# Five, four, three and two rows of wo to a transfer in place of three and two

## The chip, the core and the metric

The kernel runs on one core of a Trainium2 chip. The metric is the device time of one launch in microseconds (us), lower is better. The profile gives one execution; the times are medians of unprofiled runs.

## The reference

One decode step for eight sequences: a layer norm, then attention over a cache with grouped heads and a dense Mish block side by side, both added to the input. Everything is float32.

```python
B, Sq, D = 8, 1, 512
Hq, Hkv, Sk, Dh = 32, 8, 8192, 128
xn = layernorm(x)
q = (xn @ wq).reshape(B, 1, 32, 128).transpose(0, 2, 1, 3)
k, v = repeat(k_cache, 4, axis=1), repeat(v_cache, 4, axis=1)
p = softmax(einsum("bhqd,bhkd->bhqk", q, k) * Dh ** -0.5)
o = einsum("bhqk,bhkd->bhqd", p, v)
A = o.transpose(0, 2, 1, 3).reshape(B, 1, 4096) @ wo
act = mish(xn @ w1 + b1)
out = x + A + act @ w2
```

The two caches are 268 MB each; wq and wo are 8 MB each, w1 and w2 3.6 MB each.

## The kernel before

The work is cut into 32 units (`UNITS`): four pairs of KV heads times eight sequences, pair by pair. A unit is one pair of heads of one sequence. Its keys are one transfer of 128 partitions by 64 KB (`load_unit(kT, ...)`, line 140) and its values another of the same size. Both go into the tile `kv`, which has one place for values (`V_AT`) and two places for keys that overlap by half (`K_AT`), so a transfer is issued only when TensorE is through with what stood there before.

The loop over `j` in line 563 is the order of the work; it is written out by hand, and each engine and the queue of SyncE (SP) take their instructions in that order. For a unit `j` it runs half of `scores(j)` (64 matmuls in all, line 329), issues the keys of `j+1`, runs the other half, `softmax(j)`, then `values(j-1)` (line 399), issues the values of `j`, prepares the key weights of `j+1`, and turns the probabilities of `j` for the next round. All loads of the caches, of wq, wo, w1 and w2 are issued by SP, so they stand in one line.

The weights wo are used after the loop. Four groups of wo, one for each pair of heads, come by transfers on 128 partitions (line 612); for the first pair only three of four column blocks come there. The fourth block of the first pair is 32 rows of four pieces of 4 KB, 512 KB in all, and comes during the loop into the tile `ws`, whose earlier content (a part of wq) is used up by then. These transfers are issued by `load_few` (line 485), which the lists `FEW1` and `FEW2` drive. An entry is (first partition, number of rows, first row, unit): in the unit named, after the values of that unit are issued, SP issues that transfer. `FEW1` has eight transfers of three rows in units 22 to 25, two in each, `FEW2` four of two rows in units 28 and 29.

In `load_few` the rows of one transfer lie four apart, in wo and in the tile alike: the transfer that begins at partition `t` fills partitions `t`, `t+4` and `t+8`. The 24 rows of `FEW1` fill partitions 0 to 11 and 32 to 43; the eight of `FEW2` then fill partitions 0 to 7, after `few(0)` (line 511) has used the first 24 at the end of unit 27. `few(1)` uses the last eight after the loop.

After the loop come `values(31)`, `few(1)`, the four groups of wo (`outputs`, line 523), and w2 in five transfers of falling size (`down_long`, line 534, and `down`, line 546), the sum with the input (line 642) and the store (line 643).

Of the kernel before, what the change touches and what calls it, by code (L numbers as in the profile page):

```python
# [65 lines left out]

FEW1 = [(32 * h + t, 3, 12 * h + t, 22 + (4 * h + t) // 2) for h in range(2) for t in range(4)]
FEW2 = [(t, 2, 24 + t, 28 + t // 2) for t in range(4)]  # L70
EARLY = 27


# [4 lines left out]
def kernel(  # L78
# [21 lines left out]
    ws = const.tile([P, CC * BW], F32, name="ws")  # L100
# [381 lines left out]
    def load_few(p, n, q):  # L482

        rows = wo[:4].rearrange("u p f -> (u p f)").rearrange("(u q i f) -> q u i f", u=4, i=4, f=BW)
        nc.sync.dma_start(
            ws[p : p + 4 * n - 3 : 4].rearrange("p (u f) -> p u f", u=4),
            rows[q : q + 4 * n - 3 : 4, :, 3],
        )

    def turn_few():  # L490
# [72 lines left out]
    for j in range(UNITS):  # L563
# [25 lines left out]
        if j == 0:  # L589
            mish(w1_t, b1_sb, kv[:, W1_AT : W1_AT + 6 * FG])  # L590
        for p, n, q, at in FEW1 + FEW2:
            if j == at:
                load_few(p, n, q)
# [14 lines left out]
    for m in range(NP):  # L608
        rows = wo[4 * m : 4 * (m + 1)].rearrange("u p f -> (u p f)")
        rows = rows.rearrange("(p f) -> p f", p=P)  # L610
        n = 3 * BW if m == 0 else 4 * BW
# [4 lines left out]
    for lo, hi in parts:  # L616
        t = kv[:, W2_AT + lo * D : W2_AT + hi * D]
# [64 lines left out]
```

## Time and profile before

| | |
|---|---|
| median of 3 runs | 1310.62 us (1310.28 to 1311.18) |
| the profiled execution's own time | 1310.38 us |
| its span, first to last instruction | 1308.6 us |
| TensorE matmul busy | 987.5 us, 75% |
| VectorE, ScalarE busy | 362.0 us, 39.3 us |
| read from memory | 561.01 MB, 429 GB/s over the span |
| the transfers of the SP queue | 99.3% of sixteen DMA engines' span |
| chain that ended last | DMA 79%, TensorE 20% |
| mean granted TensorE clock | 0.884 |

The span leaves out what lies before the first and after the last instruction, 1.8 us here. The profile counts the time that the packets of a queue took on sixteen DMA engines together, so a share of 99.3% means that on the mean the sixteen were idle for 0.7% of the span; a share of 0.0625 in a short stretch is one engine of the sixteen. TensorE is busy for three quarters of the span and waits for transfers for most of the rest.

### The profile page before, as it was taken

The page shows a single profiled execution, that of the slowest core. Times are in us where ns is not written, and L with a number is a line of the kernel's source. Part 1 is how long each engine was busy: PE and PEld are TensorE (multiplying, and loading weights), DVE is VectorE, ACT ScalarE, POOL GpSimd, SP SyncE. Part 2 cuts the span into 40 slices and gives each one's busy share as a digit, 9 for nine tenths or more (in the row PEclk, how much of TensorE's full clock was granted, in tenths as well). Part 3 has the DMA queues.
Part 4 walks back from the last instruction along what each step waited for, and adds up shares of the span by engine and source line. Part 5 has one row for each costly group of instructions (what it writes and reads, how often), then busy time and mean ns, then how long its engine had stood idle before and what let it go on. Part 6 is the DMA issues. An engine that isn't in the chain of part 4 may idle for free.

```text
span 1308.6 us, 11317 instructions
## 1 busy us (share of the span) xinstructions
PE 987.5 (75%) x5086; PEld 349.0 (27%) x5086; DVE 362.0 (28%) x771; ACT 39.3 (3%) x89; POOL 2.3 (0%) x10
## 2 busy tenths in 40 slices
PE   6967777768878668786878677688796777777677
PEld 4322222223322222232323222232232222222222
DVE  3443022230233332123331232312322330322321
ACT  1000000000000000000000000000000000000000
POOL 0000000000000000000000000000000000000000
PEclk9989888798889899878999888888897898887898
DMA  9999999999999999999999999999999999999997
GB/s 404 441 429 433 433 433 430 431 441 428 435 431 434 433 431 433 431 431 437 425 443 422 443 419 443 429 433 433 426 437 430 438 434 425 441 419 443 423 429 334
DMA packets 11608, 561.80 MB, mean 429 GB/s; under 512 B 1308, under 2 KB 1440, under 8 KB 1960
## 3 DMA queue, kind: packets, MB, share of 16 engines
q1 hardware_dynamic: 11536, 561.06, 99.3%
q8 instruction: 40, 0.66, 0.2%
q14 instruction: 8, 0.07, 0.0%
q10 hardware_dynamic: 24, 0.02, 0.0%
HBM read 561.01 MB, written 0.07 MB: 429 GB/s over the span
## 4 chain that ended last, share of the span: by engine, by line
DMA 79%; PE 20%; issue 0%; SPq 0%; DVE 0%
DMA kv<-in_v 74%; PE o L399 19%; DMA kv<-in_kT 2%; DMA kv<-in_w 2%; DMA kv<-in_wo 2%; PE s L329 1%; PE o L546 0%; SPq L134 0%; DVE os L642 0%
## 5 line engine op out<-in xcount | busy, mean ns | idle before, releaser
L329 PE MATMUL s<-kv,wk 128*64 128x512 f32 x2048 | 502.2, 653 | 180.8 <-DMA kv<-in_kT 180.8
L399 PE MATMUL o<-kv,pt 128*32 128x512 f32 x2048 | 264.5, 675 | 57.4 <-DMA kv<-in_v 57.4
L329 PEld LDWEIGHTS s<-kv,wk 128*64 128x64 f32 x2048 | 164.7, 151 | 495.0 <-issue 413.6
L341 DVE TENSOR_REDUCE nm<-s 128x1 f32<-128x512 f32 x32 | 22.1, 692 | 515.1 <-PE s L329 515.1
L368 PE MATMUL x<-e,perm 128*128 128x512 f32 x256 | 130.1, 655 | 2.0 <-ACT qr L299 2.0
L399 PEld LDWEIGHTS o<-kv,pt 128*32 128x32 f32 x2048 | 69.4, 122 | 226.1 <-issue 175.7
L407 DVE TENSOR_SCALAR os<-o,isel 128x128 f32<-128x128 f32 x32 | 11.2, 351 | 278.2 <-PE o L399 278.2
L379 DVE STREAM_TRANSPOSE tr<-x 128x512 f32<-128x512 f32 x128 | 79.2, 676 | 3.0 <-PE x L368 3.0
L368 PEld LDWEIGHTS x<-e,perm 128*128 128x128 f32 x256 | 50.6, 208 | 74.7 <-issue 72.0
L312 DVE TENSOR_TENSOR wk<-qr,mask 128x512 f32<-128x512 f32 (+1 forms) x66 | 63.5, 1003 | 18.7 <-ACT qr L299 18.7
L360 ACT ACTIVATE e<-s,nmx 128x512 f32<-128x512 f32 x32 | 22.0, 687 | 1119.8 <-DVE nmx L357 1119.8
L388 DVE TENSOR_TENSOR pt<-tr 64x512 f32<-64x512 f32 x64 | 43.9, 686 | 1.6
L384 DVE TENSOR_TENSOR tr<-tr 128x1024 f32<-128x1024 f32 x32 | 39.2, 1226 | 1.1
L409 DVE SCALAR_TENSOR_TENSOR os<-o,isel,os 128x128 f32<-128x128 f32 x96 | 33.7, 351 | 3.4
L342 PE MATMUL m<-ident,nm 128*1 128x128 f32 x32 | 8.6, 270 | 25.3 <-DVE nm L341 25.3
L353 PE MATMUL m<-ident,nx 1*128 1x1 f32 x32 | 7.0, 218 | 24.1 <-DVE nx L349 24.1
L292 PE MATMUL x<-qT,tr 128*128 128x64 f32 x128 | 19.3, 315 | 3.0 <-ACT qr L299 2.7
L292 PEld LDWEIGHTS x<-qT,tr 128*128 128x128 f32 x128 | 18.1, 226 | 6.2 <-ACT qr L299 3.3
L342 PEld LDWEIGHTS m<-ident,nm 128*1 128x1 f32 x32 | 2.5, 79 | 53.5 <-DVE nm L341 53.5
L363 DVE TENSOR_SCALAR lsel<-rsel,l 128x8 f32<-128x8 f32 x32 | 7.4, 231 | 28.8 <-ACT e L360 28.8
L416 PE MATMUL m<-hsel,os 128*128 128x8 f32 x64 | 10.9, 242 | 5.7 <-DVE rt L376 5.7
L416 PEld LDWEIGHTS m<-hsel,os 128*128 128x128 f32 x64 | 10.8, 189 | 15.3 <-issue 8.0
(106 smaller groups left out, 178.8 us busy)
## 6 DMA issues: line engine op xcount, KB each, us to landing
ws<-in_wq SPq DMA_DIRECT2D x4, 2048.0 KB, 22.6
kv<-in_wo SPq DMA_DIRECT2D x3, 2048.0 KB, 24.1
kv<-in_w SPq DMA_DIRECT2D x1, 3584.0 KB, 35.8
kv<-in_wo SPq DMA_DIRECT2D x1, 1536.0 KB
kv<-in_w SPq DMA_DIRECT2D x1, 1280.0 KB
kv<-in_w SPq DMA_DIRECT2D x1, 1024.0 KB
kv<-in_w SPq DMA_DIRECT2D x1, 768.0 KB, 34.9
kv<-in_kT SPq DMA_DIRECT2D x32, 29.4
```

The source lines that it names most:

```text
L292: nc.tensor.matmul(X[:, half, k * 64 : (k + 1) * 64], wide[:, half * 8 + k], qT, start=True, stop=True,)
L312: nc.vector.tensor_mul(w[:, i : i + n, d], q[:, i : i + n, d].to_broadcast([P, n, NH * G, REP]), mask[:, d * NH * G : (d + 1) * NH * G] .r ...
L329: nc.tensor.matmul(S[64 * c : 64 * (c + 1), :], w[:, i].rearrange("p d k h -> p (d k h)"), kk[:, i, c, :], start=(part == 0 and n == 0), s ...
L341: nc.vector.tensor_reduce(nm, S, axis=AX.X, op=ALU.max, negate=True)
L360: nc.scalar.activation(e, S, AF.Exp, bias=nmx, accum_out=l)
L368: nc.tensor.matmul(X[:, g], perm[:, g], e, start=True, stop=True)
L379: nc.vector.transpose(tr.rearrange("p (l t) c -> p t l c", t=TL)[:, tl], X.rearrange("p g (t q l) -> p t l g q", t=TL, q=PP)[:, tl],)
L384: nc.vector.tensor_add(t[:, :, 0], t[:, :, 0], t[:, :, 1])
L388: nc.vector.tensor_add(pt8[half, :, :, d * REP : (d + 1) * REP].rearrange("p c y h -> p y c h"), t[:, 0], t[:, 1],)
L399: nc.tensor.matmul(O[Q * q : Q * (q + 1), :], pt8[:, c, TL * l : TL * (l + 1), :].rearrange("p t h -> p (t h)"), vt[:, 512 * n : 512 * (n ...
L409: nc.vector.scalar_tensor_tensor(os, O[:, DH * i : DH * (i + 1)], isel[:, i : i + 1], os, op0=ALU.mult, op1=ALU.add)
L416: nc.tensor.matmul(M[:, 168 : 168 + H2], os, hsel, start=True, stop=True)
```

## The change

The same 32 rows of the same block of wo come to the same 32 partitions, by nine transfers in place of twelve. `load_few` takes consecutive rows into consecutive partitions, in place of rows four apart. Each twelve rows of `FEW1` come by transfers of five, four and three rows, in units 22 (two), 23 (two) and 24 (two), and the eight rows of `FEW2` by transfers of three, three and two rows in units 28 (two) and 29 (one).

```diff
-FEW1 = [(32 * h + t, 3, 12 * h + t, 22 + (4 * h + t) // 2) for h in range(2) for t in range(4)]
-FEW2 = [(t, 2, 24 + t, 28 + t // 2) for t in range(4)]
+FEW1 = [
+    (32 * h + lo, n, 12 * h + lo, 22 + (3 * h + t) // 2)
+    for h in range(2)
+    for t, (lo, n) in enumerate(((0, 5), (5, 4), (9, 3)))
+]
+FEW2 = [(0, 3, 24, 28), (3, 3, 27, 28), (6, 2, 30, 29)]
 EARLY = 27
...
         rows = wo[:4].rearrange("u p f -> (u p f)").rearrange("(u q i f) -> q u i f", u=4, i=4, f=BW)
         nc.sync.dma_start(
-            ws[p : p + 4 * n - 3 : 4].rearrange("p (u f) -> p u f", u=4),
-            rows[q : q + 4 * n - 3 : 4, :, 3],
+            ws[p : p + n].rearrange("p (u f) -> p u f", u=4), rows[q : q + n, :, 3]
         )
```

The instructions of TensorE, VectorE, ScalarE and GpSimd are the same in the same order; SP issues nine of these transfers where it issued twelve, and all else on its queue keeps its order.

## The prediction

> **What bounds the kernel now.** I read the page first: the slices, the queues and the chain that ended last.
>
> ```profile
> PE   6967777768878668786878677688796777777677
> DMA  9999999999999999999999999999999999999997
> q1 hardware_dynamic: 11536, 561.06, 99.3%
> q8 instruction: 40, 0.66, 0.2%
> DMA 79%; PE 20%; issue 0%; SPq 0%; DVE 0%
> ```
>
> TensorE has gaps in every slice, the DMA engines have none before the last one, and the queue that carries the loads fills 99.3% of sixteen engines' span. So time is what the DMA engines need. But a load counts only when its last engine is through, so it is the slowest engine that matters, not the mean. The stretches of the end show how unequal the sixteen are (us, busy time of TensorE and its loads, VectorE, ScalarE, GpSimd, then the granted clock, the DMA share and GB/s):
>
> ```profile
> 1296.50:1297.50 1.00, 0.89 (x9) 0.26 (x12) 0.00 (x0) 0.00 (x0) 0.00 (x0) 1.00 0.96 381
> 1297.50:1298.50 1.00, 1.00 (x12) 0.12 (x4) 0.00 (x0) 0.00 (x0) 0.00 (x0) 1.00 0.74 311
> 1303.70:1304.00 0.30, 0.04 (x4) 0.04 (x8) 0.00 (x0) 0.00 (x0) 0.00 (x0) 1.00 0.53 205
> 1304.20:1304.40 0.20, 0.20 (x16) 0.20 (x8) 0.00 (x0) 0.00 (x0) 0.00 (x0) 1.00 0.05 20
> 1304.40:1304.60 0.20, 0.20 (x16) 0.11 (x5) 0.00 (x0) 0.00 (x0) 0.00 (x0) 1.00 0.08 31
> 1304.80:1305.00 0.20, 0.20 (x9) 0.00 (x0) 0.00 (x0) 0.00 (x0) 0.00 (x0) 1.00 0.00 0
> ```
>
> About four engines have moved all their bytes at 1298 (share 0.74), eight or nine still run at 1304 (0.53), and from 1304.2 to about 1304.75 only one does (0.05 and 0.08, one of sixteen being 0.0625). The first is 7 us ahead of the last, and the last is 0.55 us behind the next. It decides when the last piece of w2 is whole, and with it the end.
>
> Now the transfers in question, from the DMA view: their sizes, and how many small packets start in short stretches (a packet of wo is 4 KB; the count under 8 KB less that under 512 B, which are completions, gives them). The stretches are 940.28 to 940.59, 940.59 to 940.90, 941.07 to 941.38, and all of 940.25 to 942.4.
>
> ```profile
> ws<-in_wo SPq DMA_DIRECT2D x8, 48.0 KB
> ws<-in_wo SPq DMA_DIRECT2D x4, 32.0 KB
> DMA packets 6, 0.14 MB, mean 449 GB/s; under 512 B 2, under 2 KB 2, under 8 KB 4
> DMA packets 9, 0.15 MB, mean 476 GB/s; under 512 B 3, under 2 KB 3, under 8 KB 7
> DMA packets 8, 0.02 MB, mean 79 GB/s; under 512 B 2, under 2 KB 2, under 8 KB 8
> DMA packets 49, 0.95 MB, mean 442 GB/s; under 512 B 12, under 2 KB 12, under 8 KB 36
> ```
>
> Two, four and six packets start in three stretches of 0.31 us: one engine, then two, then three, each at 0.155 us a packet. The 24 packets of two transfers are three engines times eight. So a transfer of three rows runs on three engines, one row (four packets, 16 KB, 0.62 us) to each, and delays those three and no other. They begin 0.31 and some 0.48 us apart. How far ahead these engines are, the chain of waits tells (start, length, what):
>
> ```profile
> 917.18 29.90 DMA kv<-in_v
> 1189.65 29.88 DMA kv<-in_v
> ```
>
> The small transfers of 940.28 stand in the queue behind the values that landed at 917.18 + 29.90 = 947.08. So the three engines had finished their share of those 6.0 to 6.8 us before the last engine: they have slack, and what they are given first costs nothing. It is used up by the end. Here is the last pair, of two rows each, in the stretches 1217.55 to 1218.30 and 1218.30 to 1219.60:
>
> ```profile
> DMA packets 7, 0.02 MB, mean 27 GB/s; under 512 B 2, under 2 KB 2, under 8 KB 7
> DMA packets 30, 0.83 MB, mean 640 GB/s; under 512 B 7, under 2 KB 7, under 8 KB 18
> ```
>
> Five packets on one engine, then its other three and eight of a second, to about 1219.6. The values before them landed whole at 1189.65 + 29.88 = 1219.53. The second engine ends its small packets when the slowest ends its load, so from here on it is itself the last, or nearly. I take it to be the one that is alone at 1304.2.
>
> Why some engines lead isn't shown outright. The 40 instruction packets of the page, 0.2% of 16 x 1308.6 us or about 1 us each, must fall on some of the engines; that would do it.
>
> **The change, part by part.**
>
> *Three issues fewer on SP.* The rows of the timeline and of line 485:
>
> ```profile
> 954.26 0.33 SPq L140 DMA_DIRECT2D kv<-in_v  x1
> 954.64 1.50 SPq L485 DMA_DIRECT2D ws<-in_wo  x2
> 973.60 0.34 SPq L140 DMA_DIRECT2D kv<-in_kT  x1
> ```
>
> The pair ends its issue at 956.14 and the next load is issued at 973.60, when its place is free. 17 us of waiting hide it: three issues fewer gain nothing, and longer ones cost nothing. The rows still come behind the same values, `few(0)` after unit 27 has them a unit earlier, `few(1)` none later. Bytes, TensorE's work and its order stay. No engine gets a new wait in front of other work.
>
> *Other engines.* With one engine to a row, as the three rows show, five rows go to five engines, the first three among them. Engine time at the old price: before, the first two had 8 + 4 = 12 rows, 12 x 0.62 = 7.4 us, the third eight, 5.0 us. Now the first and the second have nine, 5.6 us, the third eight, a fourth four, 2.5 us, a fifth two, 1.2 us. By that alone the last engine gains 1.9 us, and the end gains the 0.55 us until the next engine.
>
> [...]
>
> *Neighbouring partitions.* Before, the engines of one transfer write partitions four apart, and each keeps its 0.155 us. Now they write partitions side by side, while each engine's share of a full load is eight of 128 partitions. If neighbours have one entry into the memory that is as wide as one engine, the engines of a transfer share it. The trace has two transfers to neighbouring partitions, at the start: x (eight rows of 2 KB) and b1 (four of 1.75 KB). Their queue in the stretch 1.6 to 2.95, then that of 5.7 to 6.9 with the rate in forty slices:
>
> ```profile
> q10 hardware_dynamic: 16, 0.02, 7.6%
> GB/s 0 606 546 546 0 0 546 1152 1092 0 1698 0 546 0 60 0 1092 0 546 546 0 546 546 546 0 0 546 546 1638 0 1092 546 0 546 0 0 0 1092 546 546
> q10 hardware_dynamic: 8, 0.01, 1.7%
> ```
>
> x: 7.6% of 16 x 1.35 us is 1.64 us for eight packets, 0.2 us each, 2.6 times the 0.078 us of 2 KB at 4 KB in 0.155. b1: 1.7% of 16 x 1.2 us is 0.33 us for four, 0.08 us each, full speed; but the odd 60 in slices 2, 8, 11 and 15 shows them starting 0.09 us and more apart, never two together. So the nearer row is x, although the first reads of an execution may be slow for other reasons.
>
> The bounds, then. Below: no sharing, -0.55 us. Above: engines start each transfer together, and groups of four partitions (0 to 3, 4 to 7, 8 to 11) serve one engine's rate, so an engine needs as many times 0.62 us as there are engines in its group. First engine, per twelve rows: 4 (partitions 0 to 3) + 3 (5, 6, 7) + 3 (9, 10, 11) = 10, twice 20; then 3 (0, 1, 2) + 1 (3 alone) + 2 (6, 7) = 6; 26 x 0.62 = 16.1 us for 7.4 before, +8.7. Second: 20 + 3 + 2 + 2 = 27, 16.7 us, +9.3. The fourth comes to ten times 0.62, 6.2 us, inside its lead. Engines that wait at a foreign entry leave their own idle, so nobody gains what they lose.
>
> They don't start together: 0.31 and 0.48 us apart, 0.4 us on the mean, in which the earlier one writes alone. Nine transfers spare up to 9 x 0.4 = 3.6 us of the mean 9.0: +5.4 us. x's factor gives 9 x 0.62 x 2.6 = 14.5 us, +7.1. I take 5.5, the nearer to the working by starts. Since one of the first two engines is the last already, this reaches the end in full: the DMA row has no idle slice before the last, so even the leaders, 7 us ahead, find the next load waiting, and the last one never runs dry.
>
> [...]
>
> **The sum.** 0 (issues) + 5.5 (first two engines) on the profiled execution's 1310.38 gives 1315.9. That execution stood 0.24 below the median of three runs, 1310.62; on the median it is 1316.1.
>
> **The rivals.** *No change or a little faster: the engine is the limit, not the place it writes to.* Then the nine rows cost 5.6 us, the next engine ends the run 0.55 us earlier: 1310.1. For it: b1's packets at full speed, and 26 GB/s per engine everywhere else. It decides if an entry takes two engines' rate or more. Chance 0.21.
>
> *Sharing, but evened out by buffers.* If what waits at an entry doesn't stop its engine, each entry only sums: rows 0 to 3 twice and 0 to 3 again, twelve in all, as many as before in that group. Then the first two groups end as now: 1310.6. Chance 0.08.
>
> *Not one engine to a row.* If five rows go to one engine, the first has 2 x (5 + 1 + 1) + 3 = 17 rows, 10.5 us, +3.1: 1313.7. Against it: three rows on three engines. Chance 0.03.
>
> *The fourth engine has no lead.* At 1304 half the engines run late; if the fourth is of those, 2.5 us on it at the engine's rate moves the end by about 2: 1312.6. With sharing it stays below the first two. Chance 0.04.
>
> **How the numbers follow.** Sharing that delays the engines has 0.64, with a most likely time of 1316.1 and a range of its own from 8.7 - 9 x 0.48 = +4.4 (the larger distance of two starts) to +9.3, 1315.0 to 1319.9. The range of all goes from the first rival, less 0.3 of scatter (the three runs lie 0.9 apart), at 1309.8, to 1319.0; that leaves out only the top of the upper working. 0.2% is 2.6 us, about what a measurement of this kernel can tell from no change. Slower by more: the forecast and the third rival, 0.67. Within: the first, second and fourth, 0.33, less 0.03 for gains that I haven't found: 0.30.
>
> **What would show it.** In the trace of after: 36 small packets where there were 24, for a five- and a four-row transfer, and they last well over 0.155 us (without sharing: 0.155 us on up to five engines). The small packets of unit 29 end well after the load before them has landed. At the end one to three engines run alone for some 5 us, where it was one for 0.55. The forecast is wrong if the span stays within 1 us of 1308.6 with packets at 0.155 us, and its working is wrong if the time grows by a gap on SP, which I hold hidden, or by a load that is issued too late.

## The result and the profile after

The changed kernel takes 1315.75 us (median of six runs, 1315.13 to 1316.54) against 1310.44 us for the kernel before on the same chip: +5.3 us, a ratio of 1.004 with a 95% interval of 1.003 to 1.0051. Its profiled execution took 1315.34 us with a span of 1313.6, 5.0 more than before. The granted clock isn't what differs: its mean was 0.871 there and 0.884 before, but executions of the kernel before took 1310.28 us at 0.874 and 1310.49 at 0.872.

The page of after, the lines that answer to those shown of before:

```profile
PE   6967877778878667877868768788696678777787
DMA  9999999999999999999999999999999999999997
q1 hardware_dynamic: 11536, 561.06, 99.3%
q8 instruction: 40, 0.66, 0.2%
DMA 78%; PE 21%; issue 0%; SPq 0%; DVE 0%
```

Nothing here tells of the change: as many packets, as many bytes, the same share of busy time, over a longer span. So the same packets took longer. Where, the view by stretches shows; the 10 us in which the first small transfers come, before and then after:

```profile
938.00:948.00 10.00, 7.42 (x40) 2.37 (x40) 1.71 (x7) 0.78 (x2) 0.00 (x0) 1.00 1.01 436
938.00:948.00 10.00, 6.92 (x32) 2.23 (x28) 1.71 (x7) 0.78 (x2) 0.00 (x0) 0.94 0.98 362
```

The engines are as busy (1.01 and 0.98), but what begins in this stretch is 362 GB/s in place of 436. So short a stretch is a coarse sign; the records of the packets are a better one. Of the 64 KB packets of the large loads, 65 begin in it before, each 2.42 us long, and 53 after, 2.77 us on the mean and up to 3.30. The small packets of after, in 940.30 to 943.80 and in 945.90 to 947.90:

```profile
DMA packets 58, 1.23 MB, mean 351 GB/s; under 512 B 13, under 2 KB 13, under 8 KB 41
DMA packets 24, 0.62 MB, mean 311 GB/s; under 512 B 7, under 2 KB 7, under 8 KB 15
```

28 and 8 packets of 4 KB: the 36 of a five- and a four-row transfer. The eight at the end are the two rows of one engine that comes 5 us after the others. By the trace's records a packet of the first 24 rows lasts 0.25 us on the mean and up to 0.58, where before it lasted 0.161 and never over 0.172.

The end of after, as the end of before was shown:

```profile
1304.50:1305.50 1.00, 0.66 (x8) 0.00 (x0) 0.00 (x0) 0.22 (x1) 0.00 (x0) 1.00 0.68 274
1306.50:1307.50 1.00, 0.33 (x12) 0.33 (x16) 0.00 (x0) 0.00 (x0) 0.00 (x0) 1.00 0.23 94
1307.50:1308.50 1.00, 0.95 (x36) 0.66 (x25) 0.00 (x0) 0.00 (x0) 0.00 (x0) 1.00 0.19 74
1308.50:1309.50 1.00, 0.53 (x20) 0.53 (x24) 0.00 (x0) 0.00 (x0) 0.00 (x0) 1.00 0.11 43
1309.50:1310.50 1.00, 0.80 (x28) 0.28 (x20) 0.00 (x0) 0.00 (x0) 0.00 (x0) 1.00 0.07 23
```

Four engines, then three, two and one (0.23, 0.19, 0.11, 0.07) work alone over the last 4 us, where it was one for 0.55 us. And SP, past the second group of small transfers:

```profile
958.04 0.35 SPq L144 DMA_DIRECT2D kv<-in_v  x1
958.44 0.63 SPq L489 DMA_DIRECT2D ws<-in_wo  x2
976.57 0.35 SPq L144 DMA_DIRECT2D kv<-in_kT  x1
```

It still waits 17 us for the next place. No new wait has come.

### The profile page after: what moved, and what is told of

Its sections match the earlier page's. It is cut to its first block, busy times and chain, and to the rows that moved or that the text cites. A ratio compares the mean times of both kernels' runs of the same rounds, so it can differ in the third digit from the quotient of the medians.

```text
span 1313.6 us, 11313 instructions
## 1 busy us (share of the span) xinstructions
PE 1003.5 (76%) x5086; PEld 351.3 (27%) x5086; DVE 361.8 (28%) x771; ACT 39.4 (3%) x89; POOL 2.3 (0%) x10
## 3 DMA queue, kind: packets, MB, share of 16 engines
q1 hardware_dynamic: 11536, 561.06, 99.3%
## 4 chain that ended last, share of the span: by engine, by line
DMA 78%; PE 21%; issue 0%; SPq 0%; DVE 0%
DMA kv<-in_v 73%; PE o L403 20%; DMA kv<-in_kT 2%; DMA kv<-in_w 2%; DMA kv<-in_wo 1%; PE s L333 1%; PE o L549 0%; SPq L138 0%; DVE os L645 0%
## 5 line engine op out<-in xcount | busy, mean ns | idle before, releaser
L333 PE MATMUL s<-kv,wk 128*64 128x512 f32 x2048 | 507.8, 659 | 176.0 <-DMA kv<-in_kT 176.0
L403 PE MATMUL o<-kv,pt 128*32 128x512 f32 x2048 | 275.5, 699 | 50.8 <-DMA kv<-in_v 50.8
```

What stands on the lines that cost most here:

```text
L333: nc.tensor.matmul(S[64 * c : 64 * (c + 1), :], w[:, i].rearrange("p d k h -> p (d k h)"), kk[:, i, c, :], start=(part == 0 and n == 0), s ...
L403: nc.tensor.matmul(O[Q * q : Q * (q + 1), :], pt8[:, c, TL * l : TL * (l + 1), :].rearrange("p t h -> p (t h)"), vt[:, 512 * n : 512 * (n ...
```

## The experiments

All stand against the kernel before on the same chip, 1310.4 to 1310.6 us in each group. Below, an engine that a small transfer uses is a carrier. The engines are numbered by the size at which they come in: the first three carry transfers of three rows, the fourth those of four, the fifth those of five, and so on. An entry is what the working has partitions share: a group of four, and the group 32 further up. The engine that fills it in the full loads is its owner, the first engine for partitions 0 to 3, the second for 4 to 7, and so on. The owners are an assumption, since no trace tells which engine writes to which partitions; the runs below are read by it.

**Neighbours without larger transfers.**

```diff
-FEW1 = [(32 * h + t, 3, 12 * h + t, 22 + (4 * h + t) // 2) ...]
-FEW2 = [(t, 2, 24 + t, 28 + t // 2) for t in range(4)]
+FEW1 = [(32 * h + 3 * t, 3, 12 * h + 3 * t, 22 + (4 * h + t) // 2) ...]
+FEW2 = [(2 * t, 2, 24 + 2 * t, 28 + t // 2) for t in range(4)]
...
-            ws[p : p + 4 * n - 3 : 4]...
-            rows[q : q + 4 * n - 3 : 4, :, 3],
+            ws[p : p + n]...
+            rows[q : q + n, :, 3],
```

> The kernel before with its twelve transfers of three and two rows, same engines, same count, but the rows of one transfer in neighbouring partitions (0 to 2, 3 to 5, and so on). Theory (neighbouring partitions share one entry as wide as one engine): the first engine needs 2 x (3 + 1 + 2 + 3) + 8 = 26 times 0.62 us for 12 times before, +8.7 us, less up to 0.4 us of staggered start for each of twelve transfers, 4.8: about +4 us, 1314.5 us, packets of 0.3 to 0.5 us. Rival (the cost is that of transfers of five and four rows, which take more engines): no change, 1310.4 us, packets of 0.16 us.

Measured: 1317.5 us, ratio 1.0053 (1.0041 to 1.0066), +7.1 us, worse than the changed kernel. The small packets last 0.24 us on the mean and up to 0.51. The same engines carry as many rows in as many transfers, so the rival is out. What differs is the partitions, and with them which rows of wo one transfer reads, since neighbours in the tile are neighbours in wo; the two are told apart further down. +7.1 is nearer to the undiscounted +8.7 than to +4.

**Larger transfers without neighbours.**

```diff
+FEW1 = [(32 * h + t, n, 12 * h + t, 22 + (3 * h + t) // 2) ... for t, n in enumerate((5, 4, 3))]
+FEW2 = [(0, 3, 20, 28), (1, 3, 21, 28), (2, 2, 22, 29)]
             ws[p : p + 4 * n - 3 : 4]...
```

> The changed kernel's nine transfers of five, four, three and two rows with the rows of one transfer four partitions apart; the few rows land beside the weights they belong to, so their share of the output is left wrong, the work and the bytes are the same. Theory (entries): every engine has its own entry again, 0.16 us a packet, the first two engines have nine rows for twelve: 0 to -0.6 us against the kernel before, 1309.9 to 1310.5 us. Rival (more engines to a transfer, or an engine without slack, cost it): the changed kernel's +5 us, 1315.7 us.

Measured: 1310.44 us, ratio 1.0 (0.9991 to 1.0009). The small packets last 0.161 us again, and five, four and three rows cost nothing when they lie four apart. So it isn't the number of engines. That nothing is gained either is the fourth engine's doing. The queue of the loads has 1296 packets of 4 bytes in the traces of before and of after: sixteen for each of the 79 other transfers make 1264, and one for each of the 32 small rows the rest. I take each as the sign that one engine is through with its share, here called its completion. In this run's trace the completion of the four-row transfer that comes last, at 1025.55, is the fourth engine's. One full load takes an engine 19.35 us; followed load by load at that distance, with one step of 1.0 us, the same engine is the last at the end, 0.5 us behind the next. It takes the place of the engine that ended the run before.

**Which partitions share.** The first 24 rows in pairs 32 apart, and 64 further up:

```diff
+FEW1 = [(t, 2, t, 22 + t // 3) for t in range(12)]      # step 32 in ws, 12 in wo
```

> The first 24 rows come by twelve transfers of two rows whose partitions are 32 apart, three transfers to a unit; the last eight as in the kernel before. The first two engines carry 12 + 4 = 16 rows for 12, the third none. If partitions 32 apart share one entry: 12 x 2 + 4 = 28 times 0.62 us for 12 times, +9.9 us, less up to 0.3 us for each of twelve: about +6.4 us, 1317 us, packets of 0.3 us. If they don't: four rows more, +2.5 us, 1312.9 us, packets of 0.16 us.

Measured: 1322.85 us, ratio 1.0095 (1.0079 to 1.011), +12.5 us. The last group of these pairs, in the stretch 1065.9 to 1072.1:

```profile
DMA packets 63, 2.13 MB, mean 344 GB/s; under 512 B 8, under 2 KB 8, under 8 KB 32
```

24 packets in 6 us on two engines, 0.5 us from one to the next, where three engines needed 2.1 us for 24 before. So partitions 32 apart share: 0.5 us a packet, where rows four apart had 0.161. The size was twice what I expected; the discount for staggered starts, 3.6 us, was wrong here too, and even without it 9.9 was expected. Why it is more than that isn't shown.

```diff
-FEW1 = [(32 * h + t, 3, ...
+FEW1 = [(64 + 32 * h + t, 3, ...
```

> The kernel before with the first 24 rows written 64 partitions further up, still four apart, three to a transfer; these 24 rows meet weights of other rows, so their share of the output is left wrong. Theory (an entry serves whoever writes to it, and each entry has one engine that fills it in the full loads): the three engines now write to entries that other engines are filling at that time, packets of 0.3 us, the first two engines lose another 8 x 0.62 = 5.0 us and so do the owners of those entries, about +4.5 to +5 us, 1315 us. Rival (only engines of one transfer disturb each other): no change, 1310.4 us, packets of 0.16 us.

Measured: 1318.93 us, ratio 1.0064 (1.0051 to 1.0077), +8.5 us. The transfers read the same rows of wo as in the kernel before and lie four apart as there; only the place they write to is another. So the cost comes from where the rows are written, not from where they are read. (The last run below adds the other half: eight rows that stand side by side in wo, written four apart, cost nothing.) Carriers four apart don't disturb each other in the kernel before (0.161 us a packet), but here, by the assumed owners, they write where other engines write their full loads. That fits entries with an owner, and 8.5 us is more than the 4.5 to 5 us expected; the table under "Who pays" shows that the rest is lost by engines that carry nothing.

**Which of the two lists.** The changed kernel's `FEW1` with the `FEW2` of before, and the other way round.

> The changed kernel's transfers of five, four and three neighbouring rows for the first 24 rows, the kernel before's pairs four apart for the last eight. By the working of the prediction the first engine has 20 times 0.62 us there for 8 times before, +7.4 us, less up to 0.4 us for each of six transfers: about +5 us, 1315.4 us, so nearly all of the change lies here. Rival (the last eight rows carry it, since by then the first engines have no lead left): under +2.6 us, below 1313 us.

Measured: 1314.17 us, ratio 1.0029 (1.0018 to 1.004), +3.6 us.

> The kernel before's transfers of three rows four apart for the first 24 rows, the changed kernel's three, three and two neighbouring rows for the last eight. By the working of the prediction the first two engines have 6 or 7 times 0.62 us there for 4 times, +1.2 to +1.9 us, less up to 0.4 us for each of three: +0.4 to +1.9 us, 1310.8 to 1312.3 us. Rival (the last eight rows carry the change): above +2.6 us, over 1313 us.

Measured: 1311.34 us, ratio 1.0005 (0.9997 to 1.0014), +0.8 us, which the interval doesn't tell from none. The first 24 rows carry most of it, less than the 5 us expected; the last eight lie inside their range. The sum of the two, 4.4, is 0.9 short of the whole. The intervals are 1.4 and 1.1 us wide either way, and I don't read more into it.

**Who pays.** Nine rows, three neighbours to a transfer, into one entry; the owner varies: sixth, fifth, first and fourth engine.

```diff
+FEW1 = [(20, 3, 0, 22), (52, 3, 3, 23), (20, 3, 6, 24)]   # then 16 and 48, 0 and 32, 12 and 44
+FEW2 = []
```

> Only nine of the 32 rows come, by three transfers of three rows in units 22 to 24, all into the partitions 20 to 22 and 52 to 54, which an engine with a lead fills in the full loads; the other 23 rows are left out and the nine stand beside weights of other rows, so the output lacks them. The three carriers share with each other and with the owner: 3 x 4 x 0.62 = 7.4 us, as much as the first two engines had before, and the owner loses 5.6 us, less than its lead. If only the engines that write to an entry pay: 0 to -0.6 us, 1309.8 to 1310.4 us. If waiting writes slow the other engines too (in the trace of after their 64 KB packets stretch from 2.4 to 3.3 us at that time): +0.5 to +2 us, 1310.9 to 1312.4 us, and at the end many engines finish late together, not one.

> The same nine rows by the same three transfers as in the run with partitions 20 to 22 and 52 to 54, but into the partitions 16 to 18 and 48 to 50, whose owner I take to be an engine with a lead of 7 us; 23 rows are left out and nine stand beside weights of other rows. The carriers lose up to 7.4 us as in the kernel before, the owner 5.6 us, both inside their leads. If only the engines that write to an entry pay: 0 to -0.6 us, 1309.9 to 1310.5 us. If waiting writes slow all sixteen: +1.2 to +1.8 us (in the earlier run the engines that had nothing to do with that entry were some 1.8 us late after three transfers, less 0.55 at the end), 1311.7 to 1312.3 us, with many engines together at the end.

> The same nine rows by the same three transfers as into the partitions 16 to 18 and 48 to 50, but into 0 to 2 and 32 to 34, the entry of the first of the three carriers itself; 23 rows are left out and nine stand beside weights of other rows. In the trace, the first engine to finish the keys of unit 26 tells whether engines that write nothing small are late: it was 1037.3 us in the kernel before and 1039.2 with the entries of other engines. If waiting writes slow all sixteen wherever they wait: again 1039 us, and about +1.3 us in all. If they do so only where carriers write into the entry of an engine that isn't one of them: 1037.3 to 1037.6 us there, and 0 to -0.6 us in all, 1309.9 to 1310.5.

> The same nine rows by the same three transfers into the partitions 12 to 14 and 44 to 46, the entry of the fourth engine, which carries nothing here and has little lead; 23 rows are left out and nine stand beside weights of other rows. If it is the number of writers at one entry, or that the owner isn't a carrier, that slows all: the first engine finishes the keys of unit 26 at about 1039 us, as with the fifth and sixth engine's entries. If it is a border between the fourth and the fifth entry (a way that four engines share): 1037.3 to 1037.6 us. In all, the owner loses 5.6 us of which its lead covers about 2: some +3 to +5 us, 1313.4 to 1315.4 us, either way.

Measured: 1315.31 us (ratio 1.0035, 1.0022 to 1.0047), 1311.9 (1.0011, 1.0003 to 1.002), 1310.21 (0.9998, 0.9989 to 1.0008) and 1314.02 (1.0026, 1.0016 to 1.0037). The stretch of the first transfer, for the owners fifth and first:

```profile
938.00:948.00 10.00, 6.12 (x30) 1.95 (x26) 1.71 (x7) 0.78 (x2) 0.00 (x0) 1.00 0.99 378
938.00:948.00 10.00, 7.42 (x40) 2.31 (x38) 1.71 (x7) 0.78 (x2) 0.00 (x0) 0.91 0.98 411
```

378 GB/s against 411 by the same packets (436 before). Alone that says little: the run with five, four and three rows four apart, which lost nothing, has 415 there. But its 64 KB packets are all at 2.42 us, while with the fifth engine's entry 20 of 57 last over 2.5 us, up to 4.27, and with the first engine's 14 of 62, most of them under 2.6. What that does to the engines is worked out from the completions in the traces: when the earliest and when the latest of the sixteen finished the keys of unit 26 (us, in brackets against before), after the first lists' transfers of three units:

```
                                       earliest engine  latest engine
before                                 1037.31          1043.82
after                                  1039.63 (+2.3)   1048.77 (+4.9)
threes of neighbours                   1037.58 (+0.3)   1044.81 (+1.0)
64 further up                          1041.55 (+4.2)   1049.55 (+5.7)
nine rows, owner the sixth engine      1039.25 (+1.9)   1049.33 (+5.5)
nine rows, owner the fifth             1039.21 (+1.9)   1045.72 (+1.9)
nine rows, owner the fourth            1039.13 (+1.8)   1048.47 (+4.7)
nine rows, owner the first             1037.56 (+0.3)   1043.86 (0.0)
```

The earliest engine carries nothing small in any of these. It didn't wait for the issue either: SP issued the keys of unit 26 at least 1.8 us before the earliest engine finished the load ahead of them. Yet it is 1.8 to 4.2 us late when carriers write into the entry of an engine that isn't one of them. With threes of neighbours and with the first engine's entry, where the owner is a carrier, it is 0.3 us late; the changed kernel, at +2.3, is the exception. With the fifth engine's entry the earliest and the latest are late by the same 1.9 us. Place by place in the order of completion the sixteen are 1.7 to 2.4 us late, but for one at 4.3, and the end, 1311.9 us, is what was expected from that (1311.7 to 1312.3). The owner's own loss comes on top. The sixth and the fourth engine have little lead (by the transfers of seven rows, further down, 4.4 us and more behind the first), and in each of these two runs one engine ends alone, by 3.6 and by 2.4 us; I take it to be the owner. Here the run with the sixth, whose share falls to that of one engine (0.06):

```profile
1305.00:1306.00 1.00, 0.98 (x8) 0.00 (x0) 0.00 (x0) 0.00 (x0) 0.00 (x0) 0.78 0.39 152
1307.50:1308.50 1.00, 0.73 (x28) 0.44 (x17) 0.00 (x0) 0.00 (x0) 0.00 (x0) 1.00 0.06 25
```

That is why this run missed its expectation: I took the sixth for one with a lead. The run with the fourth engine's entry says that no border between the fourth and the fifth entry is at work: all are late there too, the earliest by 1.8 us.

**A better arrangement.** Two, both with every engine writing to its own entry only, by the assumed owners. First, two transfers of seven rows and six of three:

```diff
+FEW1 = [(t, 7, 4, 7 * t, 22) for t in range(2)]                       # partition, rows, step, row, unit
+FEW1 += [(t, 3, 4, 14 + 3 * (t - 2), 23) for t in (2, 3)]
+FEW1 += [(32 + t, 3, 4, 20 + 3 * t, 24 + t // 2) for t in range(4)]
```

> All 32 rows, every engine writing to its own entry: two transfers of seven rows and six of three rows, rows of one transfer four partitions apart; a small matrix of ones, made once at the start, puts the heads' outputs into the same order, and the last use of these rows after the loop goes away. The first three engines carry eight rows, 5.0 us, four others two, 1.2 us, all inside their leads. Theory: the engine that ended alone is 1.9 us or more earlier, the end moves to the next one, -0.5 us, 1309.9 us. Rival (what ended the run is not those engines): no change, 1310.4 us.

Measured: 1310.99 us, ratio 1.0003 (0.9994 to 1.0012): no gain. Seven rows reach the fourth, sixth and seventh engine, and by the completions of that transfer three of the seven come 4.4 to 4.9 us after the first; they have no lead to spend. Then the first three engines alone, with 11, 11 and 10 rows:

```diff
-FEW2 = [(t, 2, 24 + t, 28 + t // 2) for t in range(4)]
+FEW2 = [(0, 3, 24, 28), (1, 3, 27, 28), (2, 2, 30, 29)]               # four apart in ws, side by side in wo
```

> The kernel before with the last eight rows by transfers of three, three and two rows four partitions apart in place of four of two, so that the first three engines carry 11, 11 and 10 rows in place of 12, 12 and 8, each into its own entry; a small matrix of ones puts the heads' outputs into the same order. No row goes to the late engines that the transfers of seven rows reached. Theory (one of the first two engines ends the run, alone by 0.55 us): 0.62 us less on it, -0.5 us, 1310.0 us. Rival (the end is set by something else): no change, 1310.5 us, or the instruction fetches of the late engines decide and it scatters by that.

Measured: 1310.07 us against 1310.37, ratio 0.9997 (0.9988 to 1.0006). The end of it, 1304.00 to 1304.40:

```profile
1304.00:1304.20 0.20, 0.20 (x20) 0.11 (x12) 0.00 (x0) 0.00 (x0) 0.00 (x0) 1.00 0.24 92
1304.20:1304.40 0.20, 0.20 (x16) 0.08 (x8) 0.00 (x0) 0.00 (x0) 0.00 (x0) 1.00 0.01 0
```

No engine is alone from 1304.2 on: the one that ended the run before was one of the first two. The completions of before say the same: the last pair's second engine finishes at 1220.10, and the latest completions of the next loads follow it at 1239.44 and 1258.79, 19.35 us apart. The time is 0.3 us lower, which this measurement can't tell from none. These eight rows stand side by side in wo, as in the changed kernel, and their packets last 0.161 us: reading neighbouring rows costs nothing.

## Why the prediction was right, and where its working wasn't

*The size.* +5.5 us was forecast, +5.3 measured, 1316.1 against 1315.75. The runs with one part alone show the forecast's cause: neighbouring partitions cost without larger transfers (+7.1), larger transfers cost nothing without neighbours (0.0). The cause is the one forecast. That the total agrees to 0.2 us is in part luck: a discount that the runs refute and a loss of all engines that the working lacked nearly cancel, as the next points show.

*Three issues fewer.* Right: SP waits 17.5 us behind the second pair in both traces, and nothing came of it.

*One engine to a row.* Right: 36 packets for nine rows, and the completions of a five-row transfer come from five engines, of a seven-row one from seven. The trace of before has three rows to a transfer at most; that five go to five engines, the first three among them, was carried on from there.

*Groups of four partitions with one entry.* No run shows the groups of four, each with one engine's rate, from which the 26 and 27 shares were counted; they were assumed. What the runs show in their place: packets of neighbouring rows last 0.25 us on the mean and those of pairs 32 apart 0.5 us at the worst, in place of 0.161, at +5.3 and +12.5 us; five, four and three rows four apart last 0.161 us, at 0.0. The row of x said less than I took from it. Its mean of 0.2 us hides that five of the eight packets lasted 0.08 to 0.09 us, full speed, though seven began within 0.06 us of each other; only three lasted 0.22 to 0.48.

*Where the time is lost.* Wrong. The working put all of the cost into the small packets: 16.1 us for the first engine's nine rows, 0.45 us a packet. At 0.25 us a packet nine rows are 8.9 us, for 7.7 that twelve rows took before: about +1.1 us. The rest is in the full loads. From 915 to 1260 us the 64 KB packets of all engines exceed 2.42 us by 59 us together in after and by 9 before, while the small packets of all engines take 31.5 us for 20.6. In the three runs where every row lies in its own engine's entry the excess is 6 to 10; with nine rows in one entry it is 14 where the owner is the first engine, and 44 to 52 where it is the fifth, the fourth or the sixth.

*The start distances.* This step was wrong too. I took 0.4 us off for each transfer since the engine that comes first writes alone. I left out that the owner of the entry goes on with its full load there, and that what others put into its entry delays it: in two runs one engine, which I take to be the owner, ends alone, by 3.6 and 2.4 us. The runs with threes of neighbours (+7.1, where the discounted working gave +4 and the full one +8.7) and with pairs 32 apart (+12.5 for +6.4 and +9.9) say so. In the changed kernel the full working, +9.0, would have been 3.7 us too much. One reason is in the trace: the fourth engine's rows come 5 us late, so three writers meet where I counted four. That takes one share of 0.62 us off in each of two transfers, 1.2 of the 3.7 us. The rest stays open.

*"Delays those three and no other."* True of the kernel before, wrong of after. By the table the earliest engine, which carries nothing, is 2.3 us late at unit 26. At the end twelve of sixteen finish the last piece of w2 by 1306.79 where it was 1304.51, +2.3, and no place in the order of completion is less than 2.1 us later. The last one finishes at 1310.19 where it was 1305.19, +5.0. So nearly half of the change is lost by all sixteen engines, which my working hadn't, and the first ones end the run 2.7 us beyond that, not 5.5. The whole, as the last engine counts it, is what was forecast; who pays isn't.

*The fourth engine has no lead.* True, as the eight packets 5 us late show. As that rival's last sentence says, it stays below the first two: followed load by load as above, it finishes at 1309.05, and they at 1309.61 and 1310.19.

*The first list before the second.* Right in order, 20 of 26 shares in the first: +3.6 and +0.8, the second not told from none. One sign of the prediction failed with it: the small packets of unit 29 were to end well after the load before them, and ended 0.7 us after it, where it was 0.6 before.

## What to carry to other kernels

Where transfers bound a kernel, count engine by engine what each moves and into which partitions: an average share of 99.3% before and after hid 5 us. A small transfer between large ones is worth trying with its rows four partitions apart, and at more than one place in the tile: here five, four and three such rows cost 0.0 us, three of them 64 partitions further up 8.5 us, and neighbouring rows 5.3 and 7.1 us. And small extra work belongs on the engines that the ends of the run, looked at in stretches, show to be ahead.

## What the runs showed of the hardware that I had not expected

Small writes into one engine's entry can slow engines that write elsewhere: nine rows of 16 KB into the fifth engine's entry made the earliest and the latest of the sixteen 1.9 us late, and all others 1.7 us or more. No run shows what the engines share. What decides when all pay isn't settled: by the assumed owners, an owner outside the carriers did it four times out of four (the earliest engine 1.8 to 4.2 us late), three carriers that write into the entries of carriers alone never, in two runs (0.3 us); in the changed kernel, where every owner is a carrier but one carrier comes 5 us late, it happens too (2.3 us). The number of engines at an entry doesn't decide it: 64 further up it is only two by the same assumption, and the earliest engine was 4.2 us late.

The sixteen engines aren't equal. Seven of them lead the rest by 3 us and more when the small transfers begin, among them the first three and the fifth but not the fourth, sixth and seventh. The others fall behind by steps in their completions. In the trace of before, up to the small transfers, the sixteen together fall behind by 1.5 to 1.8 us in most full loads during which one of the 40 instruction packets begins (a few times by up to 2.7, once by 1.1), and by 0.0 to 0.1 in loads without one, but for four of 1.0. That the instruction packets cause this was not tried.

An issue of rows four apart holds SP for 0.71 us at the median, one of neighbouring rows for 0.28, from the rows of the same line in before and after:

```profile
L485 SPq DMA_DIRECT2D ws<-in_wo x12: 619/706/902, 917.6 to 1190.7; - x12
L489 SPq DMA_DIRECT2D ws<-in_wo x9: 262/281/371, 917.7 to 1194.5; - x9
```

Here it costs nothing either way, since SP waits 17 us and more behind it.
